# Splitting one block's operands ahead of the others, and loading a chunk of them at once

## The chip, the cores and the metric

The kernel runs on 1 core of one Trainium2 chip. The metric is the device time of one execution in microseconds. A core has TensorE (PE in the profile; its weight loads are a row of their own, PEld), VectorE (DVE), ScalarE (ACT), GpSimd (POOL) and SyncE (SP, which here only issues DMAs). Each engine works through its instructions in order; they wait for each other and for DMAs on semaphores.

## The reference

The network has four layers, A, B, A, B. Each adds to `x` a function of the layer norm of `x`, a matrix of 2048 positions by 512 channels.

```
x = x + A(layernorm(x)); x = x + B(layernorm(x)); x = x + A(...); x = x + B(...)

A(x):  irfft2(rfft2(x) * (w_r + i w_i))
B(u):  A = -exp(log_A_real) + i A_imag;  C = (C_real + i C_imag) * dt;  dt = exp(log_dt)
       K[d, l] = 2 Re sum_n C[d, n] exp(A[d, n] dt[d] l)        # 128 modes n, l = 0 .. 2047
       y = causal convolution of u with K along l (FFT of length 4096) + u * D_skip
```

Both A layers have the same weights, and so have both B layers.

## The kernel before

**The work as a whole.** Layer A is done in three stages, each a list of steps: `A[0]` (16 rows, `spread`: layer norm and a first DFT along positions), `A[1]` (18 steps, `middle`: transform along channels in L497 to L501, the weights in L316 and L527 to L534, the transform back in L545), and `A[2]` (19 steps, `fold` and `rows_back`, the way back to rows). The convolution kernel K doesn't depend on `x`, so it is computed beside the first layer A. Then the first layer B, the second A and the second B follow.

**K's operands, `kernel_parts` (L693 to L775).** From the 128 modes of each channel, a series of steps on DVE, ACT and POOL makes five values per mode: a phase, a decay rate, the logarithm of the coefficient, a phase for longer steps, and the coefficient's phase. They lie in the tile `val` (`V`), 128 partitions (channels of a block) by 4 blocks by 5 values by 128 modes, in float32. For TensorE they are needed as bfloat16, without loss. So a *split in three parts* follows (L769 to L775): three times `V` is cast to bfloat16 (`H`, a buffer `hp` with two places, on ACT, L771), the cast is stored to a scratch tensor `parts` in DRAM (L774, SP), and, after the first two, subtracted from `V` (DVE, L773), so that the next cast takes what is left. All four blocks go through this together.

**K over time, `kernel_time` (L777 to L897).** A chunk is 32 of a block's 128 channels; 16 chunks in all, two units each. `chunk` loads a chunk's operands from `parts` into the tile `th` (two places): 96 partitions, of which the upper and the lower 48 hold two different values, each with 3 parts by 16 channels. Three slots of `th` hold the pairs of values (0, 1), (1, 2) and (3, 4). Each slot and half is a load of its own, so a chunk has six loads (L792). `grow` (L825, with the constants `kb`, loaded by POOL in L808) makes the magnitudes with Exp on ACT, `bend` (L835 to L839) the phases, `sine` and `cosine` their values, `terms` (DVE, L857 and L859) the products, `total` (PE, L870) the sum over modes, which goes to `stage` and to DRAM as `kt` (L882). `kernel_freq` later loads `kt` (L909) and transforms it block by block.

**What sets the order.** Steps are Python functions that issue instructions; `interleave` mixes lists of them in proportion to their lengths. `steps` gives a generator such as `kernel_parts` as a list of 10 calls, one for each stretch up to a `yield`:

```
made = self.steps(kernel_parts, ...)   # [step] * 10
interleave(A[0][:PC])                  # 4 rows
interleave(A[0][PC:], made)            # 12 rows with the 10 steps
interleave(K[:cuts[0]], A[1])          # 31% of K with layer A's middle
interleave(K[cuts[0]:cuts[1]], A[2])
```

A scheduler then decides, from that order and a model of each instruction's duration, where each instruction stands on its engine; on the chip that order is fixed. Nearly all DMAs are issued by SP, in its order: the loads of `x` (L408) and of layer A's weights (`wt`, L513), the stores to `parts`, the operand loads, and the stores and loads of `kt` and of layer A's result (`h`, L603).

Of the kernel before, what the change touches and what calls it, by code (L numbers as in the profile page):

```python
# [12 lines left out]
ALU = mybir.AluOpType  # L13
PSUM = bass.MemoryType.PSUM
PI = np.pi
LN2 = float(np.log(2))
MAGIC = 1.5 * 2.0 ** 23

NW = '000'
POS = 3  # L20
# [39 lines left out]
KP = 0  # L60
# [186 lines left out]
class Net:  # L247
# [11 lines left out]
    def steps(self, f, *a):  # L259

        it = []

        def step():
            if not it:
                it.append(f(*a))
            next(it[0], None)

        return [step] * 10

    @contextmanager  # L270
    def phase(self, name, space=bass.MemoryType.SB, side="left", **tags):
# [111 lines left out]
    def layer_a(self, w, x=None, src=None, dst=None):  # L383
# [109 lines left out]
        def forward(q):  # L493
# [18 lines left out]
            W = self.sb("wt", [2, 257])  # L512
            self.dma("L")(W, w[q])  # L513
            e = copies[we]
# [162 lines left out]
    def exp(self, x, tmp):  # L677
# [3 lines left out]
        nc.vector.tensor_scalar(x, x, -150.0, 150.0, op0=ALU.max, op1=ALU.min)  # L681
        nc.vector.tensor_scalar(k, x, 1.4426950408889634, MAGIC, op0=ALU.mult, op1=ALU.add)
        nc.vector.tensor_scalar_add(k, k, -MAGIC)
        nc.vector.scalar_tensor_tensor(x, k, -0.693359375, x, op0=ALU.mult, op1=ALU.add)
# [8 lines left out]
    def kernel_parts(self, kin, log_dt, parts, blks, *tags):  # L693

        nc = self.nc
        BF = mybir.dt.bfloat16
        I32 = mybir.dt.int32
        D, G = nc.vector, nc.gpsimd  # L700
        n = len(blks)
        raw, V = (self.sb(t, [n, c, 128]) for t, c in zip(tags, (4, 5)))
        S = self.sb(tags[2], [7, n, 128])
        nc.sync.dma_start(raw, kin[:, blks.start:blks.stop])
        if blks.start == 0:

            self.ld, self.dt = self.sb("ld", [4]), self.sb("dt", [4])
            nc.sync.dma_start(self.ld, log_dt)
            D.tensor_copy(self.dt, self.ld)
        ld, dt = (t[:, blks.start:blks.stop] for t in (self.ld, self.dt))  # L710
        s = [S[:, i] for i in range(7)]
        re, im, C = raw[:, :, 0], raw[:, :, 1], raw[:, :, 2:4]
        cr, ci = C[:, :, 0], C[:, :, 1]
        yield

        sw, u, mx, mn, rc, ph, lm = s
        nc.scalar.activation(sw, cr, ACT.Abs)
        nc.scalar.activation(u, ci, ACT.Abs)
        D.tensor_max(mx, sw, u)
        D.tensor_tensor(mn, sw, u, op=ALU.min)  # L720
        D.tensor_scalar_max(rc, mx, 1e-30)
        D.reciprocal(rc, rc)
        G.tensor_mul(mn, mn, rc)
        yield
        nc.scalar.activation(ph, mn, ACT.Arctan)
        D.tensor_tensor(sw, u, sw, op=ALU.is_gt)
        for sign, c in ((sw, PI / 2), (None, PI)):
            if sign is None:
                sign = sw
                D.tensor_scalar(sign, cr, 0.0, None, op0=ALU.is_lt)  # L730
            G.tensor_scalar(u, ph, -2.0, c, op0=ALU.mult, op1=ALU.add)
            G.tensor_mul(u, u, sign)
            G.tensor_add(ph, ph, u)
        D.tensor_scalar(sw, ci, 0.0, -2.0, op0=ALU.is_lt, op1=ALU.mult)
        G.tensor_mul(u, sw, ph)
        G.tensor_add(ph, ph, u)
        yield

        e = rc.bitcast(I32)
        D.tensor_scalar(e, mx.bitcast(I32), 23, None, op0=ALU.logical_shift_right)  # L740
        D.tensor_scalar(mx.bitcast(I32), mx.bitcast(I32), 0x7FFFFF, 0x3F800000, op0=ALU.bitwise_and, op1=ALU.bitwise_or)
        nc.scalar.activation(mx, mx, ACT.Ln)
        nc.scalar.activation(mn, mn, ACT.Square)
        nc.scalar.activation(mn, mn, ACT.Ln, bias=1.0)
        L = V[:, :, 2]
        D.scalar_tensor_tensor(L, e, LN2, mx, op0=ALU.mult, op1=ALU.add)
        D.scalar_tensor_tensor(L, mn, 0.5, L, op0=ALU.mult, op1=ALU.add)
        D.scalar_tensor_tensor(L, L, -126 * LN2, ld[:, :, None].to_broadcast([128, n, 128]), op0=ALU.add, op1=ALU.add)
        yield

        if blks.start == 0:
            self.exp(self.dt, self.sb("dt3", [3, 4]))
        dtb = dt[:, :, None].to_broadcast([128, n, 128])
        D.scalar_tensor_tensor(im, im, 1 / (2 * PI), dtb, op0=ALU.mult, op1=ALU.mult)
        D.tensor_scalar(lm, im, MAGIC, -MAGIC, op0=ALU.add, op1=ALU.add)
        D.tensor_sub(im, im, lm)
        yield
        D.tensor_scalar_mul(V[:, :, 0], im, -0.5)
        for c, o in ((64.0, V[:, :, 3]), (32.0, u)):
            D.tensor_scalar_mul(lm, im, c)  # L760
            D.tensor_scalar(lm, lm, MAGIC, -MAGIC, op0=ALU.add, op1=ALU.add)
            D.scalar_tensor_tensor(o, im, c, lm, op0=ALU.mult, op1=ALU.subtract)
        D.tensor_add(u, u, V[:, :, 0])
        D.scalar_tensor_tensor(V[:, :, 4], ph, 1 / (2 * PI), u, op0=ALU.mult, op1=ALU.add)
        yield
        self.exp(re, S[:, 2:5])
        D.scalar_tensor_tensor(V[:, :, 1], re, -1.0, dtb, op0=ALU.mult, op1=ALU.mult)
        yield
        for part in range(3):  # L769
            H = self.sb(tags[3], [n, 5, 128], dt=BF)  # L770
            nc.scalar.copy(H, V)  # L771
            if part < 2:
                D.tensor_sub(V, V, H)  # L773
            nc.sync.dma_start(parts[blks.start:blks.stop, :, part].rearrange("b q r n -> r b q n"), H)  # L774
            yield  # L775

    def kernel_time(self, parts, kt, units, group):  # L777

        nc = self.nc
        BF = mybir.dt.bfloat16  # L780
# [3 lines left out]
        KQ, RM, RN, KP, RP = (KB[:, k:k + 512] for k in range(0, 2560, 512))  # L784
# [1 line left out]
        live = {}  # L786

        def chunk(blk, ch):
            th = self.sb("th", [3, 2, 128], dt=BF, rows=96)
            for slot, q in enumerate((0, 1, 3)):  # L790
                for i in range(2):
                    self.dma("C")(th[48 * i:48 * i + 48, slot],  # L792
                                      parts[blk, q + i, :, 32 * ch:32 * ch + 32].rearrange("p (c h) n -> p c h n", h=2))
            state["th"] = th

        def ordered(*a, **k):
# [7 lines left out]
        def grow(i):  # L804

            h = i % 2
            if i == units[0]:
                nc.gpsimd.dma_start(KB, self.cst["kb"])  # L808
                state["ni"] = self.sb("ni", [128], dt=BF)
                nc.gpsimd.dma_start(state["ni"], self.cst["ni"])  # L810
            if h == 0:
                chunk(i // 8, i // 2 % 4)
            th = state["th"]
            mag = self.sb("mag", [3, 512])
            for k, (slot, c) in enumerate(((0, RM), (0, RN), (1, RP))):
                if k == 1 and RNP[i % len(RNP)] != "a":

                    e = nc.gpsimd if RNP[i % len(RNP)] == "g" else nc.vector
                    t = self.sb("e32", [16], 2)
                    m = mag[:, 0].rearrange("p (d b) -> p d b", b=32)  # L820
                    e.tensor_mul(t, m[:, :, 31], m[:, :, 1])
                    e.tensor_mul(mag[:, 1].rearrange("p (d b) -> p d b", b=32), m, t[:, :, None].to_broadcast([128, 16, 32]))
                    continue
                p = self.ps("pk", [512])
                nc.tensor.matmul(p, th[:, slot, h], c, start=True, stop=True)  # L825
                ordered(mag[:, k], p, ACT.Exp)
            live[i] = mag, th

        def bend(i, j):

            h, e = i % 2, slice(256 * j, 256 * j + 256)
            mag, th = live[i]
            whole = self.sb("kw", [512], dt=BF)
            p = self.ps("pk", [2, 256])
            nc.tensor.matmul(p[:, 0], th[:, 0, h], KQ[:, e], start=True, stop=False, skip_group_check=True)  # L835
            nc.tensor.matmul(p[:, 1], th[:, 2, h], KP[:, e], start=False, stop=False, skip_group_check=True)
            p = p.rearrange("p k d -> p (k d)")
            nc.vector.tensor_scalar(whole, p, MAGIC, -MAGIC, op0=ALU.add, op1=ALU.add)
            nc.tensor.matmul(p, state["ni"], whole, start=False, stop=True, skip_group_check=True)  # L839
            live[i, j] = p, mag  # L840
# [47 lines left out]
        for now, units_then in zip(halves, groups[1:] + [[]]):  # L888
            n = len(now)
# [207 lines left out]
def net_kernel(ctx, tc, x, w, ends, kin, log_dt, d_skip, out, **cst):  # L1097
    nc = tc.nc
    net = Net(ctx, tc, cst)
    kt = net.dram.tile([2048, 512], F32, name="kt")  # L1100
    parts = net.dram.tile([4, 5, 3, 128, 128], mybir.dt.bfloat16, name="parts")
    kf = net.dram.tile([4, 4, 2, 128, 512], F32, name="kf")
    hd, hd2 = (net.dram.tile([128, 16, 512], F32, name=n) for n in ("h1", "h2"))
    xv = x.rearrange("(p n) d -> p n d", n=16)
# [8 lines left out]
    with ExitStack() as outer:  # L1113
        with ExitStack() as early:
# [65 lines left out]
            for b in range(EF, 4):  # L1180
                i = 2 * b - EF - 1
# [3 lines left out]
        h = net.h  # L1185
# [41 lines left out]
```

## Time and profile before

| | |
|---|---|
| time, median of 3 runs | 787.24 us |
| the 3 runs | 787.24, 789.84, 782.07 us |
| span of the profiled execution, first to last instruction | 781.1 us |
| the profiled execution's own time | not given on the page; the span is 1.0 us below the fastest run |
| busy share of the span | DVE 83%, PE 80%, PEld 57%, ACT 55%, POOL 52% |
| mean granted TensorE clock | 0.934 |
| DMA | 144923 packets, 80.64 MB |
| operand loads (L792) | 96, 24 KB each |
| stores of the parts (L774) | 3, 640 KB each |

A page gives the busy time of each engine over one execution, and the costliest groups of instructions by line, output and input. The trace behind it can be asked for more: the busy time in any stretch of the span, who waited for whom and how long, and the instructions in order of time. In such an answer a row of the timeline has its start, its duration, engine, line, operation, output and input, and in brackets the idle time before it with what ended that. A row of the waits has the waiting instruction, what released it, the total, the number of times and the longest. Where rows of a line or a tile are asked for, three durations are its shortest, median and longest in ns. `xN` after a row means N instructions in one.

### The profile page before, as it was taken

To read this page: it belongs to the slowest core of one execution; us is meant where nothing else is said; L and a number is where in the kernel's file an instruction comes from. 1 tells how busy PE (TensorE), PEld (TensorE's weight loads), DVE (VectorE), ACT (ScalarE), POOL (GpSimd) and SP (SyncE) were. 2 spreads that over 40 slices of the span, in tenths; PEclk is the share of its full clock that TensorE was granted. 3 is DMA by queue.
4 is the path that set the end of the run, shared out by engine and by line. 5 is a ranking of instruction groups with operands and counts; after the bars stand their busy time and mean duration, and the time that the engine had idled before them with its cause. 6 is when DMAs were issued, how large, how long until landed. Compare 5 with 4: busy or idle time off the path is not lost. (4 is left out here: it accounts for less than half of the span.)

```text
span 781.1 us, 18929 instructions
## 1 busy us (share of the span) xinstructions
PE 627.7 (80%) x7248; PEld 443.5 (57%) x7248; DVE 649.3 (83%) x1301; ACT 428.1 (55%) x919; POOL 404.9 (52%) x596
## 2 busy tenths in 40 slices
PE   3447888897867977998889887874899896989986
PEld 2336666665534543656365656654777663566766
DVE  7998748979998999769996997878578696889992
ACT  3433778854748765887568834323756336242312
POOL 3675876764825245721657266281055572475760
PEclk9998899999979997999989999997999999799998
DMA  8300552344546503452325539422133114234513
GB/s 311 128 0 1 129 138 56 110 75 151 114 167 184 137 9 64 124 145 82 51 68 117 192 55 257 141 95 69 55 82 83 28 28 136 70 95 120 154 29 83
DMA packets 144923, 80.64 MB, mean 103 GB/s; under 512 B 78561, under 2 KB 124513, under 8 KB 143937
## 3 DMA queue, kind: packets, MB, share of 16 engines
q1 hardware_dynamic: 144576, 78.90, 36.2%
q8 instruction: 58, 0.95, 0.5%
q0 software_dynamic: 256, 0.52, 0.4%
q14 instruction: 33, 0.26, 0.1%
HBM read 54.89 MB, written 25.03 MB: 102 GB/s over the span
## 5 line engine op out<-in xcount | busy, mean ns | idle before, releaser
L974 POOL TENSOR_TENSOR u<-wb,wb 64x512 f32<-64x512 f32 x90 | 129.2, 1436 | 85.2 <-DVE wb L962 75.9
L316 PE MATMUL p<-z,mb 128*64 128x512 f32 (+2 forms) x480 | 102.0, 535 | 8.3 <-DVE wb L962 5.4
L870 PE MATMUL pv<-qp 128*64 128x128 f32 x1024 | 78.9, 295 | 11.4 <-DVE qp L859 6.9
L859 DVE TENSOR_TENSOR qp<-qp,mag 128x1024 f32<-128x1024 f32 x64 | 83.8, 1317 | 1.0
L962 DVE TENSOR_TENSOR wb<-p,kk 128x512 f32<-128x512 f32 x128 | 80.6, 674 | 4.7 <-PE p L316 4.6
L870 PEld LDWEIGHTS pv<-qp 128*64 128x64 f32 x1024 | 62.0, 147 | 38.8 <-ACT stage L878 10.2
L648 ACT COPY z<-p 128x512 f32<-128x512 f32 x96 | 51.4, 597 | 58.1 <-PE p L316 43.7
L316 PE MATMUL p<-mb,u 128*64 128x64 f32 x2048 | 72.9, 235 | 10.6 <-DVE u L974 4.5
L316 PEld LDWEIGHTS p<-mb,u 128*64 128x64 f32 x2048 | 70.7, 150 | 18.7 <-issue 11.3
L857 DVE SCALAR_TENSOR_TENSOR qp<-qp,mag 128x256 f32<-128x256 f32 x128 | 64.8, 523 | 13.6 <-ACT qp L800 13.3
L654 DVE STREAM_TRANSPOSE z<-z 128x512 f32<-128x512 f32 x96 | 58.5, 673 | 18.0 <-ACT z L648 18.0
L527 DVE TENSOR_TENSOR w<-wt,p 128x514 f32<-128x514 f32 x64 | 42.6, 686 | 33.3 <-PE p L316 18.6
L1086 POOL TENSOR_SCALAR w<-w,norms 128x128 f32<-128x128 f32 x64 | 40.5, 647 | 51.9 <-DMA w<-h 28.3
L532 POOL TENSOR_TENSOR w<-w,w 64x257 f32<-64x257 f32 x48 | 40.1, 835 | 50.3 <-DVE w L527 46.2
L456 PE MATMUL p<-w,w 128*128 128x128 f32 x128 | 32.0, 429 | 40.8 <-DVE w L449 30.8
L987 ACT COPY u<-p 128x512 f32<-128x512 f32 x64 | 37.6, 590 | 43.8 <-PE p L316 43.8
L316 PEld LDWEIGHTS p<-z,mb 128*64 128x64 f32 x480 | 34.2, 140 | 37.0 <-issue 20.2
L456 PEld LDWEIGHTS p<-w,w 128*128 128x128 f32 x128 | 27.8, 318 | 44.7 <-issue 24.8
L800 ACT ACTIVATE kf<-pk 128x512 f32<-128x512 f32 x64 | 38.9, 608 | 24.1 <-PE pk L839 23.6
L316 PE MATMUL p<-t,w 64*64 64x128 f32 x1024 | 43.3, 290 | 5.8 <-issue 2.6
L974 DVE TENSOR_TENSOR u<-wb,wb 64x512 f32<-64x512 f32 x38 | 46.9, 1234 | 0.5
L800 ACT ACTIVATE qp<-kf,half 128x512 f32<-128x512 f32 x64 | 47.2, 737 | 0.1
(200 smaller groups left out, 1495.3 us busy)
## 6 DMA issues: line engine op xcount, KB each, us to landing
wt<-in_w SPq DMA_DIRECT2D x32, 257.0 KB
kf<-kk SPq DMA_DIRECT2D x32, 256.0 KB
kk<-kf SPq DMA_DIRECT2D x32, 256.0 KB
u<-in_x SPq DMA_DIRECT2D x16, 256.0 KB
hr<-in_x SPq DMA_DIRECT2D x16, 256.0 KB
kt<-stage SPq DMA_DIRECT2D x32, 128.0 KB
h<-hr SPq DMA_DIRECT2D x16, 256.0 KB
w<-kt SPq DMA_DIRECT2D x32, 128.0 KB
```

The lines of the kernel that those rows point to most:

```text
L316: last = self.nc.tensor.matmul(out, weights, data, start=not more, stop=True, skip_group_check=True).ins
L456: nc.tensor.matmul(p[:, b], xf[:, b], t, start=True, stop=True)
L527: nc.vector.tensor_mul(m[pl], W, px[:, None, :].to_broadcast([128, 2, 257]))
L648: nc.scalar.copy(tiles["z"][:, :, :, b, m:m + 2].rearrange("p u j m r -> p (u j) (m r)"), ps[b].rearrange("p u j m r -> p (u j) (m r)"))
L654: nc.vector.transpose(tiles["zt"][:, u:u + 8].rearrange("p u j d -> p (u j d)"), tiles["z"][:, u:u + 8].rearrange("p u j b m r -> p (u j b ...
L800: last["x"] = nc.scalar.activation(*a, **k).ins
L857: nc.vector.scalar_tensor_tensor(QP[:, c, 0], QP[:, c, 1, :, ::-1], -1.0 if c else 1.0, m[:, 0], op0=ALU.mult, op1=ALU.mult)
L859: nc.vector.tensor_mul(t, t, mag[:, None, 1:3, 256 * j:256 * j + 256].to_broadcast([128, 2, 2, 256]))
L870: nc.tensor.matmul(p[64 * t:64 * t + 64, g], QP[:, c, 2, d:d + 2].rearrange("p s a -> p (s a)"), QP[:, c, 0:2, d:d + 2].rearrange("p k s b ...
L962: nc.vector.tensor_mul(split(m[c, pl], "du", [32, 16]), by_channel(p), split(k[c], "du", [32, 16]))
L974: self.added = e[0].tensor_sub(y[0:64], v[0, 0], v[1, 1]), e[1].tensor_add(y[64:128], v[0, 1], v[1, 0])
L1086: (self.nc.gpsimd if XNE[k] == "g" else self.nc.vector).tensor_scalar(t[:, k], t[:, k], scale, bias, op0=ALU.mult, op1=ALU.add)
```

## The change

The five values are put in another order in `V`, so that the slots of `th` are two overlapping runs of three: values 0 to 2 and 2 to 4. The scratch `parts` is laid out as block, run, part, channel, three values, modes, with value 2 stored in both runs. A chunk (2 runs by 3 parts by 16 channels on 96 partitions, two channels by three values by 128 modes on each) is then one load with pieces of 1536 bytes instead of six loads with pieces of 512 bytes. The split is done for block 0 first and for blocks 1 to 3 together afterwards, each with three casts, two subtractions and six stores (two per part). The generator has 13 stretches instead of 10, so 13 steps are mixed with the 12 rows.

```diff
+BLKS = [slice(0, 1), slice(1, 4)]
...
-        return [step] * 10
+        return [step] * 13
...
-        L = V[:, :, 2]
+        L = V[:, :, 4]
...
-        for c, o in ((64.0, V[:, :, 3]), (32.0, u)):
+        for c, o in ((64.0, V[:, :, 1]), (32.0, u)):
...
-        D.scalar_tensor_tensor(V[:, :, 4], ph, 1 / (2 * PI), u, op0=ALU.mult, op1=ALU.add)
+        D.scalar_tensor_tensor(V[:, :, 3], ph, 1 / (2 * PI), u, op0=ALU.mult, op1=ALU.add)
...
-        D.scalar_tensor_tensor(V[:, :, 1], re, -1.0, dtb, op0=ALU.mult, op1=ALU.mult)
+        D.scalar_tensor_tensor(V[:, :, 2], re, -1.0, dtb, op0=ALU.mult, op1=ALU.mult)
         yield
-        for part in range(3):
-            H = self.sb(tags[3], [n, 5, 128], dt=BF)
-            nc.scalar.copy(H, V)
-            if part < 2:
-                D.tensor_sub(V, V, H)
-            nc.sync.dma_start(parts[blks.start:blks.stop, :, part].rearrange("b q r n -> r b q n"), H)
-            yield
+        for bs in BLKS:
+            v = V[:, bs]
+            for part in range(3):
+                H = self.sb(tags[3], [bs.stop - bs.start, 5, 128], dt=BF)
+                nc.scalar.copy(H, v)
+                if part < 2:
+                    D.tensor_sub(v, v, H)
+                for i in range(2):
+                    nc.sync.dma_start(parts[bs, i, part].rearrange("b r s n -> r b (s n)"),
+                                      H[:, :, 2 * i:2 * i + 3].rearrange("p b s n -> p b (s n)"))
+                yield
...
-            th = self.sb("th", [3, 2, 128], dt=BF, rows=96)
-            for slot, q in enumerate((0, 1, 3)):
-                for i in range(2):
-                    self.dma("C")(th[48 * i:48 * i + 48, slot],
-                                      parts[blk, q + i, :, 32 * ch:32 * ch + 32].rearrange("p (c h) n -> p c h n", h=2))
+            th = self.sb("th", [2, 3, 128], dt=BF, rows=96)
+            self.dma("C")(th, parts[blk, :, :, 32 * ch:32 * ch + 32].rearrange("i p (c h) s n -> (i p) c (h s n)", h=2))
...
-            for k, (slot, c) in enumerate(((0, RM), (0, RN), (1, RP))):
+            for k, (slot, c) in enumerate(((0, RM), (0, RN), (2, RP))):
...
-                nc.tensor.matmul(p, th[:, slot, h], c, start=True, stop=True)
+                nc.tensor.matmul(p, th[:, h, slot], c, start=True, stop=True)
...
-            nc.tensor.matmul(p[:, 0], th[:, 0, h], KQ[:, e], start=True, stop=False, skip_group_check=True)
-            nc.tensor.matmul(p[:, 1], th[:, 2, h], KP[:, e], start=False, stop=False, skip_group_check=True)
+            nc.tensor.matmul(p[:, 0], th[:, h, 0], KQ[:, e], start=True, stop=False, skip_group_check=True)
+            nc.tensor.matmul(p[:, 1], th[:, h, 1], KP[:, e], start=False, stop=False, skip_group_check=True)
...
-    parts = net.dram.tile([4, 5, 3, 128, 128], mybir.dt.bfloat16, name="parts")
+    parts = net.dram.tile([4, 2, 3, 128, 3, 128], mybir.dt.bfloat16, name="parts")
```

## The prediction

> **What bounds the kernel now.** I read the page first, then the busy time in stretches, then the waits, and last the timeline around the places that the diff touches.
>
> ```profile
> span 781.1 us, 18929 instructions
> PE 627.7 (80%) x7248; PEld 443.5 (57%) x7248; DVE 649.3 (83%) x1301; ACT 428.1 (55%) x919; POOL 404.9 (52%) x596
> ...
> 40.00:60.00 20.00, 9.25 (x36) 8.04 (x36) 20.00 (x46) 5.72 (x17) 14.70 (x23) 1.00 0.00 0
> 60.00:80.00 20.00, 14.15 (x77) 11.63 (x76) 17.53 (x32) 9.29 (x24) 10.73 (x22) 0.83 0.02 2
> 80.00:100.00 20.00, 16.03 (x99) 12.60 (x100) 13.94 (x17) 13.84 (x28) 16.34 (x34) 0.83 0.65 150
> 100.00:120.00 20.00, 17.68 (x125) 13.26 (x126) 8.85 (x15) 15.30 (x38) 15.67 (x39) 0.91 0.49 116
> 120.00:140.00 20.00, 17.91 (x139) 13.03 (x139) 18.11 (x29) 18.34 (x43) 12.31 (x28) 0.91 0.19 55
> 140.00:160.00 20.00, 17.67 (x170) 13.19 (x170) 15.45 (x22) 16.43 (x37) 15.20 (x22) 1.00 0.31 101
> ```
>
> No engine bounds the whole. DVE (third pair of a stretch: us busy of 20) is full from 40 to 60, where the modes and layer A's first stage share it. From 80 to 120 it stands 17.2 us of 40 (6.06 + 11.15): layer A's middle runs alone there, and the modes' time kernel (K, `kernel_time`), which is mostly DVE work, hasn't begun. From 100 on PE is at 88 to 90% in every stretch, so a step that slips is made up only slowly. The change works on the moment when K begins (105 us) and on SP's queue afterwards.
>
> ```profile
> PEld L825 <- DMA th<-parts: 2.8, 1, 2.8
> PE pk L825 <- DMA kb<-in_kb: 1.7, 1, 1.7
> PE pk L825 <- DMA th<-parts: 0.6, 1, 0.6
> PEld p L316 <- DMA w<-kt: 2.5, 2, 1.3
> PE p L316 <- DMA w<-kt: 1.5, 2, 1.0
> POOL w L1086 <- DMA w<-h: 26.3, 7, 14.7
> ```
>
> These are all waits from 100 to 450 us that a transfer near the change could shorten (total, times, longest). PE waits for operand loads at the first chunk alone; the other fifteen chunks are in time. That already caps what the loads can give.
>
> **Part 1, six loads become one.** 96 issues become 16.
>
> ```profile
> L792 SPq DMA_DIRECT2D th<-parts x96: 682/684/857, 100.8 to 406.8; - x96
> ...
> 100.76 8.91 SPq L792 DMA_DIRECT2D th<-parts  x12
> ...
> 104.95 0.94 PE L545 MATMUL p<-ca,w 128*128 128x128 f32 x6
> 107.58 0.38 PE L825 MATMUL pk<-kb,th 96*128 96x512 bf16 x1 [1.70 <-DMA kb<-in_kb]
> 108.58 0.46 PE L825 MATMUL pk<-kb,th 96*128 96x512 bf16 x1 [0.62 <-DMA th<-parts]
> 109.27 0.64 PE L497 MATMUL p<-ca,x 128*128 128x132 f32 x2
> ```
>
> SP saves 80 x 0.684 = 54.7 us of issuing, nearly all beside work of others. On PE, the time from 105.89 (104.95 + 0.94) to 109.27 goes to K's first two matmuls and their waits: 1.70 for the constants `kb`, 0.62 more for the second part of the operands. The weight-load wait of 2.8 overlaps these two. One load has no late second part: I take -0.6. Bounds: 0, if the one load lands as late, and -3.4 (the whole gap, 109.27 - 105.89), if `kb` is in time too. In the built order `kb`'s issue on POOL and its first use both move up by one of layer A's steps, so I leave its 1.7 in place.
>
> Later SP's relief matters where something urgent stands behind a chunk:
>
> ```profile
> 233.25 4.39 SPq L792 DMA_DIRECT2D th<-parts  x6
> 237.68 2.62 SPq L909 DMA_DIRECT2D w<-kt  x4
> ```
>
> The loads of the finished time kernel (`w<-kt`) start right after six operand loads; with one they could start 3.7 us sooner (4.39 - 0.68). PE's waits for them are 2.5 and 1.5, all together 4.0, so the bounds are -4.0 and 0; I take -1.5, since one wait of each pair follows such a group. POOL's 26.3 for `w<-h` is mostly idle time of an engine that is 52% busy: 0.
>
> The Trainium skill (DMA: Bandwidth & Descriptors, "Rules for kernel authors") says that many small transfers should be merged, and that below 64 KB one pays mostly overhead. By it, with that page's about 2 us for each, an estimated 160 us would be at stake for 80 loads if each were waited for, and the span would be near 620; by the waits above it is 3.4 at most for the first chunk, so I give that no chance.
>
> **Part 2, the split in two blocks.** Three casts and two subtractions of 2560 columns become six and four, of 640 and 1920.
>
> ```profile
> 78.17 2.33 ACT L771 CAST hp<-val 128x2560 bf16<-128x2560 f32 x1
> 78.86 0.64 POOL L532 TENSOR_TENSOR w<-w,w 64x257 f32<-64x257 f32 x1 [7.40 <-DVE w L527]
> 81.02 2.82 DVE L773 TENSOR_TENSOR val<-val,hp 128x2560 f32<-128x2560 f32 x1
> 81.26 3.08 POOL L532 TENSOR_TENSOR w<-w,w 64x257 f32<-64x257 f32 x1
> 83.87 2.33 ACT L771 CAST hp<-val 128x2560 bf16<-128x2560 f32 x1 [1.29 <-DVE val L773]
> 86.53 2.83 DVE L773 TENSOR_TENSOR val<-val,hp 128x2560 f32<-128x2560 f32 x1
> 93.72 2.33 ACT L771 CAST hp<-val 128x2560 bf16<-128x2560 f32 x1
> ...
> L774 SPq DMA_DIRECT2D parts<-hp x3: 378/385/389, 80.5 to 96.1; - x3
> ```
>
> By columns a cast is 0.6 and 1.75 us, a subtraction 0.7 and 2.1; with some 0.1 more for each extra instruction ACT pays +0.3, DVE +0.2, both inside engines with idle time. POOL's L532 takes 3.08 beside the long subtraction against 0.64 alone; behind it stands layer A's step. With 2.1 in place of 2.8 this is 0.7 shorter, twice, and one small subtraction costs it 0.7: together -0.5 (bounds -1.4 and +0.7).
>
> What is added is a wait. The buffer `hp` has two places, so cast n waits until the stores of cast n - 2 have landed. Before, only the third cast had such a wait, and it found the store long done. Now casts 3 to 6 have it. The casts 2, 3, 4 stand close together on ACT, so cast 4 asks for the stores of cast 2 some 1.4 us after that cast. How long does a landing take at that place?
>
> ```profile
> kb<-in_kb POOLq DMA_DIRECT2D x1, 480.0 KB, 5.1
> ni<-in_ni POOLq DMA_DIRECT2D x1, 32.0 KB, 4.9
> ```
>
> Even 32 KB took 4.9 us when DMA was half busy. So cast 4 waits up to 4.9 + 0.4 - 1.4 = 3.9 us. Behind it on ACT stand the copies of layer A's third step (L507, L511), for which PE's L316 waits, and DVE's L527 for that. Casts 5 and 6 are a step of layer A further apart and should find their stores landed. I take +2.5, bounds 0 and +8 (two such waits).
>
> The Trainium skill (DMA: Bandwidth & Descriptors, "Anatomy of one DMA") speaks against such a wait on a store: it puts about 2.0 us on every transfer whatever its size, most of it the confirmation from the target memory, with HBM as the slowest target. By its 2.0 the wait of cast 4 would be an estimated 1.0 and the span 1.5 less than mine; the rows of this trace, 4.9 and 5.1, are longer, and I go by them.
>
> **Part 3, order and queue.** The number of turns goes from 10 to 13, so the modes' steps come earlier between layer A's rows. In the built order of DVE, layer A's last row now has three instructions of the modes behind it instead of eight:
>
> ```profile
> 70.02 0.54 DVE L449 SCALAR_TENSOR_TENSOR w<-w,lnn 128x128 f32<-128x128 f32 x1
> ...
> 74.90 0.69 DVE L764 SCALAR_TENSOR_TENSOR val<-tmp 128x512 f32<-128x512 f32 x1
> ...
> 73.21 0.81 PE L497 MATMUL p<-ca,x 128*128 128x132 f32 x2 [0.46 <-ACT x L458]
> ...
> 99.94 0.39 PE L497 MATMUL p<-ca,x 128*128 128x132 f32 x2
> 102.94 0.39 PE L497 MATMUL p<-ca,x 128*128 128x132 f32 x2
> ```
>
> DVE is full there and its work is unchanged, so the modes still end at 75.6 (74.90 + 0.69). The three last take 3 x 0.69 = 2.1, so the last row ends at 73.5 instead of 70.6, and the middle starts at 76.1 instead of 73.2: +3.0. Against it, K's first matmul stands after 8 of layer A's middle steps instead of 9; a step is 3.0 (102.94 - 99.94): -3.0. So K begins at the same time, with layer A one step behind. The operand loads stand behind all twelve stores and one weight load on SP, not behind block 0's six: what block 0 gains by going first is given back there.
>
> Farther on, K's instructions stand up to 48 matmuls earlier among layer A's and B's on PE, from 140 to 240 us, so some of DVE's idle time where layer A's last stage begins could be filled:
>
> ```profile
> DVE w L582 <- ACT w L579: 4.4, 1, 4.4
> ```
>
> I take -1.5, bounds -4.4 and +4 (as much lost elsewhere by an order that fits less well). After about 240 us the orders are nearly the same.
>
> **Sum.** -0.6 - 1.5 - 0.5 + 2.5 + 3.0 - 3.0 - 1.5 = -1.6: a span of 779.5. The page gives no time of its own for the profiled execution; its span is 1.0 below the fastest run (782.07) and 6.1 below the median (787.24). With the 6.1, the median becomes 785.6.
>
> **Rivals.** *K sets the end, and block 0 is early.* Alone, the split of block 0 takes 3 x 0.6 + 2 x 0.7 = 3.2 us of ACT and DVE instead of 3 x 2.33 + 2.82 + 2.83 = 12.6. If K began these 9.4 us sooner, in DVE's 17.2 idle us, all that K bounds would move: -9.4 - 1.5 - 1.5 = -12.4, 774.8. For it: the DVE column; against it: the loads' place on SP and K's place on PE.
>
> *Slower: ACT stands at the casts.* If landings take the 4.9 of the small row for the stores too, casts 4, 5 and 6 each stand up to 3.9, layer A is 3.0 late from the start, and PE at 88% doesn't catch up: 3 x 3.9 + 3.0 - 1.5 = +13.2, 800.4. It decides once a store lands later than 2.5 us after its cast, for from there every cast is met. For it: 4.9 and 5.1; against it: the spacing of casts 5 and 6.
>
> *Nothing:* the loads are hidden anyway and the orders come out even: 787.2.
>
> **How the numbers follow.** Forecast 785.6: 0.45. K early: 0.2. ACT at the casts: 0.25. Nothing: 0.1. One per cent, about what a measurement of this kernel can tell from no change, reaches from 779.4 to 795.1. Faster: most of the second case and a little of the forecast, 0.21; slower: four fifths of the third case and a little of the forecast's upper bounds, 0.25; within: 0.54. The forecast's own range is 779 to 793; to leave out no more than 2 in 10 it goes to 773 and 801.
>
> **What would show it.** Right: 16 operand loads near 0.7 us each; PE's L825 without a wait for them, but with one for `kb`; the first L497 near 76 and the first L825 near 105; one cast with idle time of 2 to 4 us before it on ACT; K's DVE work (L838) beginning near 119. Wrong towards faster: the first L825 before 100. Wrong towards slower: casts 5 and 6 waiting too, or the first L825 after 109. If the first half agrees and the time doesn't, the cause lies in the order from 140 to 240 us.

## The result, and the profile after

| | before | after |
|---|---|---|
| median of 15 runs each, us | 786.43 (777.92 to 790.42) | 795.63 (791.17 to 798.83) |
| ratio after to before | | 1.0131, 95% interval 1.0106 to 1.0156 |
| profiled execution, us (its span) | not on record (781.1) | 793.43 (791.7) |

The changed kernel is slower by 1.3%, some 10 us; forecast was a gain of 1.6. Here and below a median is over all executions of a kernel, while a ratio leaves out those more than 1.5% above the fastest of their kernel, so it can differ from the quotient of two medians. In every execution whose span is on record the time is 1.7 to 2.1 us above the span, so the profiled execution of before took an estimated 783 us and is not the run of 782.07. The head of the changed kernel's page:

```profile
span 791.7 us, 18817 instructions
...
PE 631.8 (80%) x7248; PEld 444.4 (56%) x7248; DVE 646.9 (82%) x1303; ACT 428.8 (54%) x922; POOL 419.0 (53%) x596
```

The engines have hardly more instructions: DVE is busy 2.4 us less than before, ACT 0.7 more, PE 4.1 more at equal counts, POOL 14.1 more at equal counts. What grows is idle time (span less busy time): by 13.0 us on DVE, 9.9 on ACT, 6.5 on PE. So the loss is mostly waiting. First the timeline, the groups, the waits and the DMA issues at the places that the diff touches (columns as in the views of before):

```profile
L796 SPq DMA_DIRECT2D th<-parts x16: 715/762/897, 97.8 to 414.3; - x16
...
75.55 0.81 PE L499 MATMUL p<-ca,x 128*128 128x132 f32 x2 [0.46 <-ACT x L460]
...
83.72 1.79 ACT L775 CAST hp<-val 128x1920 bf16<-128x1920 f32 x1 [0.21 <-DMA parts<-hp]
90.25 1.79 ACT L775 CAST hp<-val 128x1920 bf16<-128x1920 f32 x1
94.27 1.79 ACT L775 CAST hp<-val 128x1920 bf16<-128x1920 f32 x1
...
81.44 0.63 POOL L534 TENSOR_TENSOR w<-w,w 64x257 f32<-64x257 f32 x1 [7.64 <-DVE w L529]
85.00 0.81 POOL L534 TENSOR_TENSOR w<-w,w 64x257 f32<-64x257 f32 x1 [0.51 <-DVE w L529]
85.88 3.15 POOL L535 TENSOR_TENSOR w<-w,w 64x257 f32<-64x257 f32 x2
92.14 2.15 POOL L517 COPY wt<-ends 128x4 f32<-128x4 f32 x1
...
108.15 1.01 PE L828 MATMUL pk<-kb,th 96*128 96x512 bf16 x2 [3.87 <-DMA kb<-in_kb]
...
119.69 1.29 DVE L841 TENSOR_SCALAR kw<-pk 128x512 bf16<-128x512 f32 x2 [0.35 <-PE pk L839]
```

```profile
PEld p L318 <- DMA w<-kt: 1.4, 4, 0.5
PE p L318 <- DMA w<-kt: 0.5, 2, 0.3
```

```profile
parts<-hp SPq DMA_DIRECT2D x6, 288.0 KB, 3.4
parts<-hp SPq DMA_DIRECT2D x6, 96.0 KB, 1.7
kb<-in_kb POOLq DMA_DIRECT2D x1, 480.0 KB, 7.3
```

Up to 120 us things stand nearly where the prediction has them: sixteen operand loads of 0.76 us, no wait for them on PE, the middle of layer A from 75.55 (76.1 forecast), K's first rounding on DVE (L841) at 119.69 (119 forecast, 119.14 before). So the loss lies later.

Where it lies was hard to read from two profiles. The eight transposes with which a block of layer B's `forward_b` begins on DVE (L654, now L656) make good landmarks. Those of `kernel_freq` block 0, of the first input block and of `kernel_freq` block 1, before and then after:

```profile
256.25 4.85 DVE L654 STREAM_TRANSPOSE z<-z 128x512 f32<-128x512 f32 x8
277.49 4.85 DVE L654 STREAM_TRANSPOSE z<-z 128x512 f32<-128x512 f32 x8
331.32 4.86 DVE L654 STREAM_TRANSPOSE z<-z 128x512 f32<-128x512 f32 x8 [3.84 <-ACT z L648]
```

```profile
272.55 4.85 DVE L656 STREAM_TRANSPOSE z<-z 128x512 f32<-128x512 f32 x8
292.65 4.86 DVE L656 STREAM_TRANSPOSE z<-z 128x512 f32<-128x512 f32 x8 [4.22 <-ACT z L650]
340.97 4.87 DVE L656 STREAM_TRANSPOSE z<-z 128x512 f32<-128x512 f32 x8 [4.57 <-ACT z L650]
```

Block 0 is 16.3 us late, and block 1 still 9.6. That gave my first theory: the new order puts K's next units ahead of block 0's rows on PE, and these set the end. It was wrong, as the next section shows.

### The profile page after: what moved, and what is told of

The parts are those of the page before. It is cut to its first block, busy times and chain, and to the rows that moved or that the text cites. A ratio compares the mean times of both kernels' runs of the same rounds, so it can differ in the third digit from the quotient of the medians.

```text
span 791.7 us, 18817 instructions
## 1 busy us (share of the span) xinstructions
PE 631.8 (80%) x7248; PEld 444.4 (56%) x7248; DVE 646.9 (82%) x1303; ACT 428.8 (54%) x922; POOL 419.0 (53%) x596
## 5 line engine op out<-in xcount | busy, mean ns | idle before, releaser
L977 POOL TENSOR_TENSOR u<-wb,wb 64x512 f32<-64x512 f32 x90 | 128.4, 1427 | 84.0 <-DVE wb L965 73.5
L318 PE MATMUL p<-z,mb 128*64 128x512 f32 (+1 forms) x480 | 103.6, 544 | 10.8 <-DVE wb L965 5.8
L965 DVE TENSOR_TENSOR wb<-p,kk 128x512 f32<-128x512 f32 x128 | 80.8, 675 | 4.5 <-PE p L318 3.3
L862 DVE TENSOR_TENSOR qp<-qp,mag 128x1024 f32<-128x1024 f32 x64 | 82.2, 1287 | 1.2
L860 DVE SCALAR_TENSOR_TENSOR qp<-qp,mag 128x256 f32<-128x256 f32 x128 | 67.0, 539 | 16.3 <-ACT qp L803 15.9
L1089 POOL TENSOR_SCALAR w<-w,norms 128x128 f32<-128x128 f32 x64 | 52.5, 835 | 50.3 <-DMA w<-h 42.3
L318 PEld LDWEIGHTS p<-mb,u 128*64 128x64 f32 x2048 | 68.1, 146 | 18.4 <-issue 10.3
L318 PE MATMUL p<-mb,u 128*64 128x64 f32 x2048 | 70.4, 231 | 9.5 <-DVE u L977 4.2
L656 DVE STREAM_TRANSPOSE z<-z 128x512 f32<-128x512 f32 x96 | 58.5, 674 | 23.5 <-ACT z L650 23.5
L534 POOL TENSOR_TENSOR w<-w,w 64x257 f32<-64x257 f32 x48 | 36.1, 752 | 53.9 <-DVE w L529 44.9
L318 PEld LDWEIGHTS p<-z,mb 128*64 128x64 f32 x480 | 35.8, 143 | 41.3 <-issue 21.6
L841 DVE TENSOR_SCALAR kw<-pk 128x512 bf16<-128x512 f32 x64 | 42.9, 680 | 9.8 <-PE pk L839 9.6
L547 PE MATMUL p<-ca,w 128*128 128x128 f32 x256 | 40.6, 289 | 9.3 <-POOL w L535 4.0
L977 DVE TENSOR_TENSOR u<-wb,wb 64x512 f32<-64x512 f32 x38 | 47.0, 1236 | 0.5
```

What stands on the lines that cost most here:

```text
L318: last = self.nc.tensor.matmul(out, weights, data, start=not more, stop=True, skip_group_check=True).ins
L656: nc.vector.transpose(tiles["zt"][:, u:u + 8].rearrange("p u j d -> p (u j d)"), tiles["z"][:, u:u + 8].rearrange("p u j b m r -> p (u j b ...
L860: nc.vector.scalar_tensor_tensor(QP[:, c, 0], QP[:, c, 1, :, ::-1], -1.0 if c else 1.0, m[:, 0], op0=ALU.mult, op1=ALU.mult)
L862: nc.vector.tensor_mul(t, t, mag[:, None, 1:3, 256 * j:256 * j + 256].to_broadcast([128, 2, 2, 256]))
L965: nc.vector.tensor_mul(split(m[c, pl], "du", [32, 16]), by_channel(p), split(k[c], "du", [32, 16]))
L977: self.added = e[0].tensor_sub(y[0:64], v[0, 0], v[1, 1]), e[1].tensor_add(y[64:128], v[0, 1], v[1, 0])
```

## Experiments

All ratios are to the kernel before on the same chip (785.6 to 786.1 us in the five sets of runs). "K" is the time kernel; counts of K's PE instructions contain weight loads.

**One half of the change at a time, and the place at 240 us by itself.** e1 is the changed kernel with `BLKS = [slice(0, 4)]` and ten turns. e2 is the kernel before with the split's loop:

```
+        for bs in BLKS:
+            v = V[:, bs]
...
+                nc.sync.dma_start(parts[bs, :, part].rearrange("b q r n -> r b q n"), H)
...
-        return [step] * 10
+        return [step] * 13
```

> Only the new scratch layout: one load a chunk instead of six, the split still done for all four blocks together, ten turns. Built so, the first rows of layer B's kernel transform (kernel_freq, block 0) stand on PE behind 384 of K's PE instructions (weight loads counted), before 374, in the changed kernel 404. Order theory (the time goes to where these rows stand behind K): 786 to 789 us, first row matmul of layer B within 4 us of before's 240.96. Rival layout (the single load itself costs the time, by landing later or loading the DMA queues): near the changed kernel's 796. Rival split (blocks, casts and turns cost it): 786, without layer B coming late.

> Only the split of block 0 ahead of blocks 1 to 3, with thirteen turns; old scratch layout with six loads a chunk. Built so, layer B's first rows stand behind 336 of K's PE instructions, earlier than before's 374. Order theory: no later than before, 780 to 787 us. Rival layout: 786. Rival split, or layer A's middle being late by 6 us and carried to the end: 792 to 796.

Measured: e1 798.53 us, 1.0175 (1.0145 to 1.0206); e2 801.34 us (six runs, 790.32 to 802.42), 1.0163 (1.0104 to 1.0222). Each half alone costs as much as both together. Two costs of 1.6% that add up to 1.3% are not costs of the halves' work.

e3 and e4 move the four row steps of `kernel_freq` block 0 alone; `issue_after` queues an instruction behind another on its engine without a wait. e3, on the changed kernel:

```
-            interleave(K[at:done], sum(F[EF - 1], []) + first[0] + first[1])
+            rest = sum(F[EF - 1], []) + first[0] + first[1]
+            for f in rest[:4]:
+                f()
+                K[at:] = [partial(behind, net.multiplied, k) for k in K[at:]]
+                interleave(K[at:at + 2])
+                at += 2
+            interleave(K[at:done], rest[4:])
```

e4, on the kernel before, wraps each `f()` in `issue_after` of K's last matmul instead and lets 3, 11, 5 and 4 steps of K pass behind the rows.

> The changed kernel whole, with one thing set by hand: the four row steps of kernel_freq for block 0 are queued on PE ahead of the K steps that before had behind them (372 of K's PE instructions ahead of the first row, before 374, changed kernel 404). Everything of the change stays in: layout, split, turns, 3.9 us wait for kb, layer A's middle 6 us late. Order theory: the time returns to before's, 784 to 788 us, first row matmul near 241. Rivals layout, split, or a late middle of layer A: it stays at 793 to 797.

> The kernel before with nothing of the change, but with the same row steps of kernel_freq queued on PE behind as many K steps as in the changed kernel (410 ahead of the first row; the changed kernel has 404). Order theory: 793 to 798 us, with layer B's first row matmul at 250 to 254 and the end as late as in the changed kernel. Any rival that puts the time on layout, split or layer A's middle: 786, since none of them is in it.

Measured: e3 793.48 us, 1.0119 (1.0089 to 1.0150); e4 785.08 us, 0.9981 (0.9952 to 1.0010). The theory falls twice. DVE in e4:

```profile
266.34 4.86 DVE L654 STREAM_TRANSPOSE z<-z 128x512 f32<-128x512 f32 x8 [1.08 <-ACT z L648]
286.20 4.86 DVE L654 STREAM_TRANSPOSE z<-z 128x512 f32<-128x512 f32 x8 [4.21 <-ACT z L648]
330.86 4.86 DVE L654 STREAM_TRANSPOSE z<-z 128x512 f32<-128x512 f32 x8 [1.04 <-ACT z L648]
```

The rows come 10 us late and block 1 is in time all the same. My reading, which no run tests, is that K goes ahead while block 0's rows wait, and block 1 needs K. In e3 block 0's transposes begin 21 us before the changed kernel's, and nothing measurable comes of it:

```profile
251.24 4.85 DVE L657 STREAM_TRANSPOSE z<-z 128x512 f32<-128x512 f32 x8
...
335.02 4.86 DVE L657 STREAM_TRANSPOSE z<-z 128x512 f32<-128x512 f32 x8 [5.62 <-ACT z L651]
```

**Work and order apart.** The scheduler derives each queue's order anew for every kernel. The next kernels take it out of its hands: a list of both kernels' common instructions is kept, and each is queued behind the one ahead of it in the list. Casts, subtractions and stores of the split are in no list. The kernel before wasn't run with the list of its own order, so a price of the list itself isn't measured; e6, in the changed kernel's list, is no slower than the changed kernel without one.

```
+def queue(tc):
+    by = {i.name: i for i in tc.nc.cur_bb.bb.instructions}
...
+            if before is not None:
+                tc.add_manual_dep(i, before.name, mybir.DependencyInfo(mybir.DependencyClass.NoSync,
+                                                                       mybir.DependencyReason.DATA))
+            before = i
```

> The changed kernel's work (new layout, one load a chunk, six casts, twelve stores), with every engine's queue put in the order of the kernel before: each instruction that both kernels have is queued behind the one that stands ahead of it there; only casts, subtractions and stores of the split are left to the scheduler. Theory order (the change costs time only through the order that the scheduler derived for it): 781 to 788 us. Rival work (loads, stores, casts or the layout cost it by themselves): 793 to 797.

> The reverse: the work of the kernel before (three casts over all blocks, six loads a chunk, old layout), with every engine's queue in the order of the changed kernel. Theory order: 793 to 799 us. Rival work: 784 to 788. If both matter: about 790 here and in the run with the orders the other way round.

> The changed kernel's work, with all queues in the order of before up to the first row of layer B's kernel_freq (about 240 us), and in the changed kernel's own order for the rest. If the loss comes from how K is set among layer A's last two stages (100 to 240 us): 782 to 788. If it comes from the order behind 240 us: 793 to 798.

> The counterpart: the changed kernel's work in its own order up to the first row of layer B's kernel_freq, and in the order of before for the rest. If the loss comes from 100 to 240 us: 793 to 798. If it comes from the order behind 240 us: 782 to 788.

| kernel | work of | order | us | ratio (95%) | last products to block 2's transposes, us |
|---|---|---|---|---|---|
| after | after | after | 795.63 | 1.0131 (1.0106 to 1.0156) | 19.67 |
| e6 | before | after | 793.13 | 1.0097 (1.0063 to 1.0131) | 20.27 |
| e7 | after | before to 240 us, then after | 793.78 | 1.0106 (1.0067 to 1.0146) | 19.66 |
| e12 | after | before, but after from 370 to 465 | 792.76 | 1.0081 (1.0047 to 1.0116) | 20.29 |
| e14 | after | after, but before from 370 to 465 | 788.48 | 1.0047 (1.0015 to 1.0078) | 15.82 |
| e5 | after | before | 789.26 | 1.0047 (1.0013 to 1.0081) | 15.46 |
| e8 | after | after to 240 us, then before | 789.80 | 1.0033 (0.9994 to 1.0072) | 15.95 |
| e11 | after | before, but after from 240 to 370 | 789.76 | 1.0029 (0.9988 to 1.0070) | 15.45 |
| e13 | before | before (unchanged) | 787.06 | 1.0019 (0.9982 to 1.0055) | 15.82 |

e12, e14, e11 and e13 are told of below, the last column too. Order theory holds for e6; in e5 two thirds of the loss are gone and not all, so it falls between its two ranges. e7 and e8 put the order's part behind 240 us, though e8 is 1.8 us above its range of 782 to 788. It was then split at products of `weigh` (L962, now L965), and the two halves of the change were put into before's order:

> Only the new scratch layout with one load a chunk, the split over all blocks at once, and every queue in the order of before. The whole change in that order took 789.3 (+0.5%). If those 3 us come from the layout or the one load: 788 to 790. If from the split: 785 to 787. If the layout is a gain that the split hides: 782 to 785.

> Only the split of block 0 ahead of the others, with the six loads and the layout of before, and every queue in the order of before. If the 3 us of the change's work come from the six casts, four subtractions and their stores: 788 to 790. If from the layout: 785 to 787.

> The change's work in the order of before, except from the first row of layer B's kernel_freq (about 240 us) to the fifteenth product of weigh (about 370 us), where it has the changed kernel's order. Theory two places (ACT, in order, stands at copies and activations of K that wait for PE, once between 240 and 345 us and once between 375 and 420): 3 to 5 us above the 789.3 of the whole change in before's order, 792 to 794; ACT's waits for PE at K's stage copies and activations together 16 to 21 us between 235 and 345, where before's order has 10 to 12. Rival one place at 375: 789.

> As the last, but with the changed kernel's order only from the fifteenth to the thirty-fifth product of weigh (about 370 to 465 us). Theory two places: 2.5 to 4 us above 789.3, 792 to 793; ACT's waits for PE at K's activations 8 to 9 us between 374 and 425 where before's order has 4.5. Rival one place at 240: 789.

Measured: e9 788.08 us, 1.0032 (0.9997 to 1.0067); e10 791.17 us, 1.0063 (1.0032 to 1.0094). In before's order the halves stand a third of a per cent and two thirds above the kernel before, where the scheduler's own orders gave 1.75 and 1.63. e11 costs nothing above e5, against the expectation (its ACT does wait 18.8 us there, and it is made up); e12 costs 3.5 us above e5 (0.34%, within the scatter of one such pair, so the next run was needed). Of the two places expected only the second costs time.

**What the window does.** In the changed order one pair of products on DVE is followed by a longer way to the transposes of `kernel_freq` block 2. DVE, PE and ACT there, the changed kernel first:

```profile
412.19 1.27 DVE L965 TENSOR_TENSOR wb<-p,kk 128x512 f32<-128x512 f32 x2
...
420.91 0.67 DVE L841 TENSOR_SCALAR kw<-pk 128x512 bf16<-128x512 f32 x1
...
431.86 4.86 DVE L656 STREAM_TRANSPOSE z<-z 128x512 f32<-128x512 f32 x8 [5.13 <-ACT z L650]
...
421.64 0.38 PE L842 MATMUL pk<-kw,ni 128*128 128x512 bf16 x1 [2.88 <-DVE kw L841]
...
422.63 2.08 PE L318 MATMUL p<-mb,u 128*64 128x64 f32 x64
...
426.51 1.59 PE L318 MATMUL p<-t,w 64*64 64x128 f32 x32
...
422.11 0.60 ACT L803 ACTIVATE kf<-pk 128x512 f32<-128x512 f32 x1 [3.17 <-PE pk L842]
```

Then e14, which is the changed kernel with before's order in this window alone:

> The changed kernel with its own order everywhere except from the fifteenth to the thirty-fifth product of weigh (about 380 to 475 us), where all queues have the order of before. Theory (there the changed order puts rows of kernel_freq, block 2, behind K's next operands on PE, and ACT and DVE wait): 3 to 4 us less than the changed kernel, 791 to 793, and no step of 3.4 us between the twenty-fifth product of weigh and the transposes of block 2 in the trace. Rival (the place only hands on a delay that comes anyway): 795 to 797.

```profile
404.46 1.27 DVE L965 TENSOR_TENSOR wb<-p,kk 128x512 f32<-128x512 f32 x2
...
411.45 0.67 DVE L841 TENSOR_SCALAR kw<-pk 128x512 bf16<-128x512 f32 x1
...
420.28 4.86 DVE L656 STREAM_TRANSPOSE z<-z 128x512 f32<-128x512 f32 x8 [1.42 <-ACT z L650]
...
411.39 1.10 PE L318 MATMUL p<-mb,u 128*64 128x64 f32 x32
412.43 0.39 PE L842 MATMUL pk<-kw,ni 128*128 128x512 bf16 x1
...
412.97 0.43 PE L318 MATMUL p<-t,w 64*64 64x128 f32 x2
```

Count from the products (412.19 and 404.46). In the changed order K's last rounding of a group (L841) stands on DVE behind one more of K's products (L862) and a sum of layer B (L977) and runs after 8.7 us, in the repaired one after 7.0. PE meets L842, which needs it, and stands 2.88 us; layer B's 64 matmuls `p<-mb,u` and the rows of block 2 (`p<-t,w`) are queued behind L842. In the repaired order these matmuls stand ahead of L842 (the last 32 at 411.39) and fill the time, and the rows begin after 8.5 us instead of 14.3. ACT stands 3.17 us for PE, and at last DVE 5.13 us instead of 1.42 for ACT's copies of the rows. From products to transposes it is 19.67 and 15.82 us: 3.9 lost. The 20 us from the products on show it too: DVE is busy 14.80 us of them in the changed kernel and 18.51 in e14, PE 16.83 and 18.93. The changed kernel first, then e14:

```profile
412.19:432.19 20.00, 16.83 (x282) 12.08 (x279) 14.80 (x20) 13.52 (x27) 17.05 (x13) 0.88 0.37 104
```

```profile
404.46:424.46 20.00, 18.93 (x312) 13.82 (x310) 18.51 (x26) 15.36 (x31) 18.18 (x17) 0.91 0.40 114
```

That the order in this window costs time is shown by the repair; which of these exchanges does it is read from two traces, and no run makes one of them alone.

The repair brings 795.63 to 788.48, more than the 3 to 4 us expected, and as far as all of before's order does (e5, 789.26). The rival that something else would hand the delay on is out. In the table the kernels fall in two classes by the last column: 19.7 to 20.3 us with ratios from 1.0081 to 1.0131, and 15.4 to 16.0 with 1.0019 to 1.0047. The three kernels with the changed work in the first class average 1.0106, the four in the second 1.0039: 0.67%, 5.3 us. The runs e9, e10, e17 and e18, which have before's order in the window too, fit in with 15.8 to 16.3 us and 1.0032 to 1.0063. Of the runs outside these lists e2 (19.67 us, 1.0163), e3 (19.68, 1.0119) and e4 (16.26, 0.9981) fit; e1 (16.90, 1.0175) doesn't.

The last four runs ask which queue does it, what comparisons scatter, and whether the order up to 300 us has a gain to be had:

> The change's work in the order of before, and only PE's queue in the changed kernel's order between those two products of weigh (103 of PE's instructions moved). If PE's queue is the cause: the step of 3.5 to 4.5 us between 388 and 418 us is there as with all queues, 791 to 794 in all. If it is ACT's or DVE's queue: no step, 788 to 790.

> The counterpart: the change's work in the order of before, and in the same window the queues of ACT, DVE, POOL and SP in the changed kernel's order, PE's in that of before. If PE's queue is the cause: no step, 788 to 790. If ACT's or DVE's is: a step of 3.5 to 4.5 us, 791 to 794.

> The kernel before, unchanged, timed against itself: what a ratio of kernels with the same order is worth. If comparisons of this kind are fair: 0.997 to 1.003, 784 to 788 us, and the 0.3 to 0.6% of the runs with the change's work in before's order are a price of that work. If it is as far off as 1.003 to 1.006, they are not.

> The changed kernel's work in its own order up to the ninth product of weigh (about 300 us), and in the order of before from there on. The repaired window alone gave 788.5. If the changed order is a little better up to 300 us and before's behind it: 783 to 786, faster than both. If nothing but the window from 370 to 465 us differs: 787 to 789.

> The same mixed order with the work of before (three casts, six loads a chunk, old layout). If the changed order is better up to 300 us: 781 to 784, faster than before. If only the window differs: 785 to 787. Against the run with the changed work it also says once more what that work costs: 0 to 3.5 us.

e15: 796.40 us, 1.0162 (1.0112 to 1.0212). e16: 800.18 us, 1.0197 (1.0134 to 1.0259). The question was put wrongly: neither queue alone is harmless. In the window e15 takes 22.86 us from products to transposes and e16 25.07, both longer than the full changed order:

```profile
409.69 1.27 DVE L965 TENSOR_TENSOR wb<-p,kk 128x512 f32<-128x512 f32 x2
...
434.76 4.86 DVE L656 STREAM_TRANSPOSE z<-z 128x512 f32<-128x512 f32 x8 [10.52 <-ACT z L650]
```

These rows are e16's. In this window a queue's order is good or bad only together with the others'.

e17: 789.68 us, 1.0054 (1.0018 to 1.0089); e18: 790.60 us, 1.0055 (1.0020 to 1.0091). In this pair, with the same order, the changed work and the old work take the same time. The other pairs of one order put the changed work higher: 0.34% for the changed kernel against e6, 0.47% for e5 against the kernel before. So the work gains nothing that shows, and a price of up to half a per cent is neither shown nor excluded. No mixture beat the kernel before. e13, the kernel before against itself, came to 1.0019 with an interval up to 1.0055, so the 0.3 to 0.6% by which the other runs with before's order in the window stand above it can't be put to a part.

## Why the prediction was wrong

- **The step that failed** is the last of Part 3: "I take -1.5, bounds -4.4 and +4", with "After about 240 us the orders are nearly the same." The sign was wrong, and so was the second sentence. The lists of e5 and e7 differ only behind 240 us, and to get from one to the other 185 of PE's 3752 listed instructions, 54 of DVE's 1299 and 58 of ACT's 894 have to be moved. From 370 to 465 us (e5 and e12) these are 36, 4 and 16; the 103 in e15's expectation doesn't come out of the lists. There a step of 3.9 us arises; repaired, the whole change is at 1.0047. I had compared the positions of K's matmuls alone; that a rounding on DVE and layer B's matmuls on PE had changed places did not show in that.
- Said rightly was only where to look: "If the first half agrees and the time doesn't, the cause lies in the order from 140 to 240 us." The order it was, but the place found lies at 412 us, some 170 us later.
- Part 1, operands: their wait on PE is gone as forecast, but `kb` took 7.3 us to land (5.1 before) and PE waits 3.87 for it instead of 1.70. So -0.6 became about +1.6. Why `kb` took longer isn't shown: the last of the twelve stores was issued by 96.98 us, 3.8 us before it. The waits for `w<-kt`, 4.0 us in the forecast, were counted twice: PE and its weight loads wait at the same two places (304.69 and 385.19). The weight loads' 2.5 became 1.4, so about -1.1 for the -1.5.
- Part 2, POOL: L534 takes 0.63 and 0.81 us, but the long rows moved on. Before, two rows of L532 took 3.08 and 3.20 us where 0.64 was usual. Now a copy takes 2.15 (0.19 is usual) and two pairs of L535 take 1.89 and 3.15 (1.34 is usual). The excess goes from 5.0 to 4.3 us, so -0.5 was near.
- Part 2, the wait at `hp`: 0.21 us instead of 2.5. The stores landed after 1.7 and 3.4 us, not 4.9; I had sized SP's stores by two loads that POOL issues. The Trainium skill (DMA: Bandwidth & Descriptors, "Anatomy of one DMA") gives about 2.0 us as the fixed part of a DMA that GpSimd issues, with a part that grows with the bytes on top. The trace has 1.7 us for SP's stores of 96 KB and 3.4 for those of 288 KB, and 7.3 for POOL's load of 480 KB.
- That Parts 1 and 2 together came out near the forecast is luck: the wait for `kb` was 2.2 us longer than taken and the wait at `hp` 2.3 shorter.
- Part 3, start of layer A's middle and of K: 75.55 and 119.69 against 76.1 and 119. Right. Layer A one step behind got no price. Its tenth step begins at 115.04 instead of 109.27, and in e8, which has the changed order up to 240 us, at 112.08; with e8 at 1.0033 it costs little.
- Rivals: "ACT stands at the casts" gave a time near the measured one for a reason that did not come: casts 5 and 6 (90.25 and 94.27) do not wait. "K early" did not come either, L828 begins at 108.15. "Nothing" is, to within half a per cent, what the change's work does (e17 and e18) and what the whole does in before's order (e5).
- Merging loads: the rule of the Trainium skill (DMA: Bandwidth & Descriptors, "Rules for kernel authors") to merge small transfers got no chance. The runs show no gain from it here: e9, with one load a chunk alone and all queues in before's order, is at 1.0032 (0.9997 to 1.0067) with 80 issues fewer.

The size is explained in part. The window accounts for some 3 of the 10 us by e12 against e5, 5 by the two classes, or 7 by the repair itself, while the step seen in the traces is 3.9. The remaining 3 to 7 us stay open; some 3 of them are at the edge of what these comparisons tell (1.0019 to 1.0063 in the runs that have before's order there). The orders of e1 and e2 were not taken apart: e1 has 16.90 us in the window (413.31 to 430.21) and must lose most of its time elsewhere.

## What to carry to other kernels

Where a scheduler orders the queues, a small edit is two changes: its work, and a new order everywhere behind it. Separate them by running the new work in the old order; here the work brought nothing that shows, and the one costly place that was found lies 300 us behind the edit. Compare landmarks over short stretches in several traces: delays of 10 and 17 us at block 0's transposes (e4 and e11) cost nothing that shows, while a step of 4 us between two later landmarks went with the loss in every kernel but e1.

## What was not expected of the hardware

Two executions of the same program differ more than many an edit moves: the 15 runs of the kernel before reach from 777.92 to 790.42 us. The second profile of the kernel before (e13) has its landmarks here, 6 us behind the first from the start of layer B on:

```profile
262.24 4.85 DVE L654 STREAM_TRANSPOSE z<-z 128x512 f32<-128x512 f32 x8
282.95 4.86 DVE L654 STREAM_TRANSPOSE z<-z 128x512 f32<-128x512 f32 x8
337.06 4.86 DVE L654 STREAM_TRANSPOSE z<-z 128x512 f32<-128x512 f32 x8 [3.41 <-ACT z L648]
```

Its mean granted clock is 0.915 against 0.934, and in the stretch from 240 to 260 us 0.75 (second row) against 0.91:

```profile
240.00:260.00 20.00, 16.94 (x255) 11.28 (x256) 16.41 (x60) 14.44 (x27) 14.51 (x24) 0.91 0.80 181
```

```profile
240.00:260.00 20.00, 16.91 (x210) 11.17 (x207) 13.15 (x60) 14.71 (x27) 13.07 (x24) 0.75 0.72 181
```

So up to 6 of the 16 us that started my first theory can be the luck of one profiled execution. The stretch in the window, by contrast, repeats to within 0.9 us in each class (15.45 to 16.33 and 19.66 to 20.29), whatever came before it.
